# A linear-attention and MLP kernel: wider warm-up products, an earlier alpha load, 32-token denominator tiles, stores by tile and a new written-out order

## The chip, the cores and the metric

The kernel runs on one core of one Trainium2 chip. The metric is the device time of one execution in microseconds (us), lower is better. The kernel before takes 114.51 us, the median of three runs from 113.99 to 115.96 us.

## The reference

There are two stages. The first is attention without a softmax, for 4 batches, 4 heads, 1088 tokens and head size 32. Each query and key gets 64 features, the outer product of two projections to 8 numbers:

```python
a = np.einsum('rd,bhsd->bhsr', S1, x)
b = np.einsum('rd,bhsd->bhsr', S2, x)
phi = np.einsum('bhsi,bhsj->bhsij', a, b).reshape(*x.shape[:-1], r * r)
...
kv = np.einsum('bhsf,bhsd->bhfd', k_p, v)
z = np.sum(k_p, axis=2)
num = np.einsum('bhsf,bhfd->bhsd', q_p, kv)
den = np.einsum('bhsf,bhf->bhs', q_p, z)[..., None] + 1e-06
return (num / den).astype(np.float32)
```

The second takes the result as 4352 tokens of 128 numbers through an MLP of width 2048, whose activation is `max(h, 0) + alpha * min(h, 0)` with one alpha per hidden unit:

```python
h = x @ w_in
g = np.maximum(h, 0.0) + alpha * np.minimum(h, 0.0)
return (g @ w_out).astype(np.float32)
```

## The kernel before, in words

All work is cut into named operations, each with the engine it runs on. The string ORDER lists them in the order in which they are emitted, as `name:engine:buffers` (p is TensorE, a ScalarE, d VectorE, g GpSimd, s the SyncE queue of DMA issues). `arrange` walks this list, so each engine's instruction stream is the list read for that engine alone. An engine works strictly in its own order: an instruction that waits holds up everything behind it on that engine. This holds for SyncE too, which issues nearly all loads and all stores. At most eight DMAs are outstanding: a further one waits until the DMA that had its semaphore eight places earlier has landed. A number behind p (`zS0:p2`) asks for fill products: matmuls of constants into a scratch bank of PSUM, 128 columns each, four of them joined to one of 512.

The names that the prediction uses, for batch b:

- `ld_*` are the loads: k, q and v of each batch (k0 in two parts, q0 in two, each v in four pieces of 32 partitions), the rows of S1 and S2, alpha, two loads of w_in, four of w_out.
- `warm` is 104 small products of constants and some larger ones at the very start (line 276 on).
- Keys: `kbT` transposes k on VectorE, `kbf` projects it on TensorE (L484), `kbfT` transposes the projection (L489), `kbp0..` form the outer products (GpSimd or VectorE), `zsb` sums the features (L508), `kvb` contracts them with v (L519), and `kvc`, `fin`, `kvR` bring kv into the form that the queries need. For batch 0 `kw`, `kwT`, `kwc` do so by a short way.
- Queries of batch 0, first half, go by their own short way in two tiles i = 0, 1: `qaa`, `qab` (L576), `qac`, `qam`, then `den` (L585, L590), `rc` (reciprocal), `rT` (spreads it, L598), `rr`, `num` (L605) and `xA`, the first finished x. All other queries: `qbf`, `q1f` .. (L443), `..p0`, `..p1`, `..PT0`, `..PT1` (L544), `..n` (L551) and `..x0`, `..x1`.
- Since max(h,0) + alpha*min(h,0) = alpha*h + (1-alpha)*max(h,0), the MLP is x times W, with W = w_in times (alpha * w_out), plus ReLU(h) times w_a, with w_a = (1-alpha) * w_out. `alT` transposes alpha on TensorE (L335), `win` casts w_in to bf16, `w_a`, `w_b`, `w_hi`, `w_lo`, `winT`, `Wmm` make w_a and W. 
- The tokens go through the MLP in groups g = 0..9: `hg.c` is one 128-wide chunk of h for 512 tokens (L641; two chunks for 256 tokens), `rg.c` its ReLU into one of ten buffers, `og.c` the product with w_a into the group's PSUM bank (L664), `Wg` the product with W, `oTg` the transpose out of PSUM (L695) and `stg.i` the stores (L705). Group 9, the last 256 tokens, leaves the transpose out (L662, L677): `oT9.0` and `oT9.1` copy it from PSUM and one store (L723) writes it.

Of the kernel before, what the change touches and what calls it, by code (L numbers as in the profile page):

```python
# [11 lines left out]
F32 = mybir.dt.float32  # L12
# [10 lines left out]
wz:g ident:g eps:d pads9:g selP:g ld_rows_1:a M2:d zero:d M64:d M4:d M8b:d warm:p ld_k0.0:s ld_rows:a ld_k0.1:s M8i:d k0T0:d:0 MZ:g rowsT:p:0 pads:g  # L23
Wk:d S2m:p:1 table:a k0f0:p:2 Sab:a k0T1:d k0f1:p ld_qa:s S2q:d ld_k1:s qaT0:d qaa0:p:4 qab0:p Wf:a qaT1:d qaa1:p:0 qab1:p k0fT0:d:0 ld_v0_2:s
identb:g ld_alpha:a zs00:p:6 k0fT1:d qac0:a:0 k1T0:d:1 zs01:p z10:a:0 qam0:d k0p4:d:0 alT:p:2 oma:d ld_v0_3:s zS0:p2 alTc:d E8:g zA:d k0p1:g
k1f0:p1:3 k0p2:d ld_v0_1:s k0p0:g zfin:p:5 qac1:a:1 zc:d ld_v0:s kv00:p:2 k0p3:g kv01:p qam1:d k1fT0:d:1 kv02:p kv03:p kv04:p kw:a den0:p:5 kwT:p
kwc:a den1:p:0 rc0:d rT0:p ld_k2:s kvc0:a:0 fin0:p ld_w_in0:s k2T0:d:2 num0:p:1 k2f0:p:3 rc1:d rr0:a:0 win0:d rT1:p ld_qb:s xA0:d h0.0a:p:5 qbT:d
k1p1:g:1 win1:a kvR0:a rr1:a:1 num1:p:7 h0.2a:p:1 r0.0a:a:0 k2fT0:d:0 r0.2a:a:1 h0.4a:p:2 ld_w_in2:s r0.4a:a:2 C0:d h0.6a:p:0 xA1:d qbf:p:3 win3:d
win2:d zs10:p:7 r0.6a:a:3 h0.8a:p:1 h0.10a:p:2 k1p0:g h0.12a:p:0 qbfT:d:0 r0.10a:a:4 z11:a:1 h0.14a:p:3 h0.0b:p:4 qbt:d:0 qbrc:d:0 ld_w_out0:s
h0.2b:p:5 qbb:d w_b0:g qbp1:d:2 r0.0b:a:5 zs20:p:6 r0.12a:a:6 ld_w_out1:s z12:a:0 winT1:p:2 zS1:p ld_w_out3:s r0.8a:a:7 ld_w_out2:s h0.4b:p:4  # L30
r0.2b:d:8 C1:a qbp0:d w_a0:g w_a2:d zS2:p w_a1:g C2:d o0.0a:p:0 o0.2a:p h0.6b:p:1 w_a3:g r0.4b:a:9 r0.14a:a:0 h0.8b:p:7 h0.10b:p:5 o0.4a:p winT0:p:4
r0.8b:a:1 o0.6a:p r0.10b:a:2 winTc0:a h0.12b:p:3 r0.12b:a:3 h0.14b:p:7 o0.8a:p ld_q1:s o0.10a:p qbPT0:d:0 o0.12a:p w_b3:g w_b1:g ld_k3:s w_hi3:a
w_lo3:g qbPT1:d o0.14a:p o0.0b:p o0.2b:p r0.6b:d:7 qbn:p:3 winTc1:d o0.4b:p o0.6b:p o0.8b:p o0.10b:p o0.12b:p w_hi0:a w_lo0:g ld_v1_2:s qbx1:a qbx0:a
# [78 lines left out]
def kernel(  # L112
# [163 lines left out]
    def warm(e):  # L276
        for i in range(104):
            nc.tensor.matmul(PS[:32, 7, :16], ones(32), ones(16), start=True, stop=True, skip_group_check=True)  # L278
        dummy(16)
# [496 lines left out]
```

## Time and profile before

| | before |
|---|---|
| median of three runs | 114.51 us (113.99 to 115.96) |
| the profiled execution | 114.77 us |
| its span, first to last instruction | 112.3 us |
| TensorE busy / weight loads | 103.9 us / 60.9 us |
| VectorE, ScalarE, GpSimd busy | 82.7, 63.2, 43.0 us |
| DMA | 11.25 MB, mean 100 GB/s |
| chain that ended last | TensorE 87%, DMA 7% |

Between the span and the execution's own time lie 2.47 us. A busy TensorE is one that has a product in flight, not one at its peak, and the granted clock (PEclk) says at which speed it then works. The times in the timeline and in the chain of waits are us from the start of the span. Many matmuls in float32 stand in the trace as two records, so a count there can be twice the count in the program.

### The profile page before, as it was taken

Reading aid. Unit: us, or ns where it says so; the run is one execution under the profiler, and the core shown is the slowest. Engines: PE = TensorE matmul, PEld = TensorE weight load, DVE = VectorE, ACT = ScalarE, POOL = GpSimd, SP = SyncE. Lnnn points to the kernel's source line nnn. Section 1 sums busy time; section 2 is a strip of 40 time slices with the busy share of each in tenths; the row PEclk is TensorE's granted clock in tenths of the full one; section 3 lists DMA queues with packets and bytes.
Section 4 is the critical chain, followed back from the end, with each engine's and each line's share of the span. In section 5 each row is a group of like instructions: output and inputs, shape, how many; then the busy total and the mean of one; then the engine's idle time right before and its main releaser. Section 6 shows DMA issues by size and latency. Waiting matters only on the chain.

```text
span 112.3 us, 3587 instructions
## 1 busy us (share of the span) xinstructions
PE 103.9 (93%) x1520; PEld 60.9 (54%) x1520; DVE 82.7 (74%) x135; ACT 63.2 (56%) x128; POOL 43.0 (38%) x48
## 2 busy tenths in 40 slices
PE   7999499999999999999999999999999999999900
PEld 7444278636687567434444743444644446878700
DVE  4274584566999799789976985879999659678600
ACT  3112202417998777942966776499754957555400
POOL 4709109895305959997099500207000000000000
PEclk9999965559999999999999999999999999999996
DMA  3999999999950000030140100052006204312431
GB/s 95 252 269 230 355 346 325 329 243 266 286 121 3 6 3 6 0 67 3 22 71 0 29 0 6 0 101 39 6 0 105 41 0 83 57 17 49 71 64 42
DMA packets 23427, 11.25 MB, mean 100 GB/s; under 512 B 17636, under 2 KB 21876, under 8 KB 23412
## 3 DMA queue, kind: packets, MB, share of 16 engines
q1 hardware_dynamic: 23300, 11.01, 39.7%
q8 instruction: 12, 0.20, 0.7%
q10 hardware_dynamic: 112, 0.02, 0.1%
q14 instruction: 3, 0.02, 0.1%
HBM read 8.80 MB, written 2.23 MB: 98 GB/s over the span
## 4 chain that ended last, share of the span: by engine, by line
PE 87%; DMA 7%; DVE 1%; ACT 0%; issue 0%
PE ps L641 28%; PE ps L664 26%; DMA al<-in_moe_alpha_dram 7%; PE ps L551 5%; PE ps L519 5%; PE ps L278 3%; PE ps L443 2%; PE ps L484 2%; PE ps L274 2%; PE ps L598 2%; PE ps L590 2%; PE ps L385 2%; PE ps L662 2%; PE ps L605 1%; PE ps L403 1%; PE ps L375 1%
## 5 line engine op out<-in xcount | busy, mean ns | idle before, releaser
L641 PE MATMUL ps<-x,w_in_bf 128*128 128x512 bf16 (+1 forms) x176 | 40.1, 333 | 0.2
L641 PEld LDWEIGHTS <-w_in_bf 128*128 128x128 bf16 x176 | 16.5, 98 | 14.9 <-issue 3.6
L664 PEld LDWEIGHTS <-w_a_bf 128*128 128x128 bf16 x160 | 15.4, 98 | 10.7 <-issue 0.7
L186 POOL TENSOR_TENSOR P__72<-Fk__70 128x1024 f32<-128x1024 f32 (+1 forms) x4 | 8.6, 2166 | 6.4 <-DVE Fk__70 L489 6.4
L652 ACT ACTIVATE rh__86<-ps 128x512 bf16<-128x512 f32 x12 | 7.2, 600 | 5.0 <-PE ps L641 4.7
L652 ACT ACTIVATE rh__87<-ps 128x512 bf16<-128x512 f32 x12 | 7.2, 601 | 3.1 <-PE ps L641 3.0
L652 ACT ACTIVATE rh__83<-ps 128x512 bf16<-128x512 f32 x10 | 6.0, 600 | 3.0 <-issue 1.2
L186 POOL TENSOR_TENSOR w_hl<-w_in_f,w_hl 128x512 bf16<-128x512 f32 x4 | 4.6, 1158 | 7.3 <-ACT w_hl L179 6.0
L652 ACT ACTIVATE rh__82<-ps 128x512 bf16<-128x512 f32 x9 | 5.4, 600 | 1.6 <-PE ps L664 1.0
L652 ACT ACTIVATE rh__88<-ps 128x512 bf16<-128x512 f32 x10 | 6.0, 600 | 0.3 <-PE ps L664 0.3
L652 ACT ACTIVATE rh__89<-ps 128x512 bf16<-128x512 f32 x9 | 5.5, 607 | 1.1 <-PE ps L641 1.1
L652 ACT ACTIVATE rh__91<-ps 128x512 bf16<-128x512 f32 x9 | 5.5, 607 | 1.0 <-PE ps L641 1.0
L652 ACT ACTIVATE rh__85<-ps 128x512 bf16<-128x512 f32 x8 | 4.8, 601 | 1.9 <-PE ps L641 1.2
L652 ACT ACTIVATE rh__84<-ps 128x512 bf16<-128x512 f32 x9 | 5.5, 606 | 0.7 <-PE ps L641 0.4
L664 PE MATMUL ps<-rh__87,w_a_bf 128*128 128x512 bf16 (+1 forms) x18 | 5.3, 332 | 0.0
L664 PE MATMUL ps<-rh__85,w_a_bf 128*128 128x512 bf16 (+1 forms) x18 | 5.3, 332 | 0.0
L664 PE MATMUL ps<-rh__83,w_a_bf 128*128 128x256 bf16 (+1 forms) x19 | 5.3, 323 | 0.0
L664 PE MATMUL ps<-rh__88,w_a_bf 128*128 128x512 bf16 (+1 forms) x17 | 5.3, 342 | 0.0
L664 PE MATMUL ps<-rh__91,w_a_bf 128*128 128x512 bf16 (+1 forms) x16 | 5.0, 341 | 0.0
L664 PE MATMUL ps<-rh__89,w_a_bf 128*128 128x512 bf16 (+1 forms) x17 | 4.9, 329 | 0.0
L186 POOL TENSOR_TENSOR w_in_f<-w_out_f,alphaT 128x512 f32<-128x512 f32 x4 | 4.2, 1066 | 1.5 <-DVE w_in_bf L181 1.5
L179 ACT CAST x<-ps 128x576 bf16<-128x576 f32 (+1 forms) x5 | 2.7, 554 | 3.5 <-PE ps L551 3.3
(206 smaller groups left out, 231.1 us busy)
## 6 DMA issues: line engine op xcount, KB each, us to landing
v<-in_v_dram SPq DMA_DIRECT2D x12, 144.0 KB, 7.8
k<-in_k_dram SPq DMA_DIRECT2D x3, 544.0 KB, 7.9
q<-in_q_dram SPq DMA_DIRECT2D x3, 544.0 KB, 7.2
w_in_f<-in_moe_w_in_dram SPq DMA_DIRECT2D x2, 512.0 KB, 8.0
w_out_f<-in_moe_w_out_dram SPq DMA_DIRECT2D x4, 256.0 KB, 7.0
out_dram<-oT__92 SPq DMA_DIRECT2D x12, 64.0 KB, 1.9
out_dram<-oT__94 SPq DMA_DIRECT2D x8, 64.0 KB, 1.9
v<-in_v_dram SPq DMA_DIRECT2D x4, 112.0 KB, 7.8
```

The lines of the kernel that those rows point to most:

```text
L179: nc.scalar.copy(dst, src)
L186: (nc.vector if e == "dve" else nc.gpsimd).tensor_tensor(out=dst, in0=a, in1=b, op=what)
L274: nc.tensor.matmul(PS[:, 7, :m], ones(128), ones(m), start=True, stop=True, skip_group_check=True)
L278: nc.tensor.matmul(PS[:32, 7, :16], ones(32), ones(16), start=True, stop=True, skip_group_check=True)
L385: nc.tensor.matmul(ps(bw)[:, :DM], winT[:, c], w_hl[:, c, y], start=c == y == 0, stop=c == NC - 1 and y == 1)
L443: nc.tensor.matmul(ps(bf)[32 * g:32 * g + 32, h, :n], Wf[32 * h:32 * h + 32, b], src[1]()[32 * h:32 * h + 32, g * n:(g + 1) * n], start=Tr ...
L484: nc.tensor.matmul(ps(bf)[32 * g:32 * g + 32, u, :n], Wk[K].rearrange("p x f -> p (x f)"), src[1]()[K, g * n:g * n + n], start=True, stop= ...
L519: nc.tensor.matmul(ps(bk)[32 * h:32 * h + 32, :R], v_sb[b][:, h, j], bview(sb(P), [[1, R]], (4 * j + h) * R), start=j == 0, stop=j == JG - ...
L551: nc.tensor.matmul(ps(bn)[32 * h:32 * h + 32, g, :n], kvR[b][32 * g:32 * g + 32, y, 32 * h:32 * h + 32], bview(sb(Q)[32 * g:32 * g + 32], ...
L641: nc.tensor.matmul(ps(b)[:, n * i:n * i + n], w_in_bf[:, c], x(), start=True, stop=True, skip_group_check=len(cs) > 1)
L652: nc.scalar.activation(dst, src, ACTF.Relu)
L664: nc.tensor.matmul(ps(bo)[:, lo:lo + n], w, rhs, start=first and lo == 0, stop=end, skip_group_check=True)
```

## The change

- `warm`: the 104 small products have 32 columns instead of 16, and behind them come one product of 512 and three of 128 columns instead of four of 512.
- alpha is loaded on ScalarE's queue right behind the rows of S1 and S2, at the start, and `alT` stands ahead of the first `k0f`. Before, its load came after the copies `Sab` and `Wf`.
- v of batch 0 is issued ahead of all later loads, and k of batch 2 is now the second key batch to be worked on (k of batch 1 was). The new lists called `aft` only record which load comes behind which; nothing in the file reads them.
- `den`: the 128 tokens of a column block are cut in four tiles of 32 instead of two of 64.
- The group of the rest (the last two 32-token columns of every batch, 256 tokens) becomes group 6 and comes ahead of the first 512 tokens of the last batch, which become group 7.
- The stores of a group stand together, right behind its `oT`. The last store is cut in two halves of 64 partitions, one on SyncE and one on ScalarE.
- ORDER is new as a whole, with more fill products: 9 units ahead of `k0f0`, 7 ahead of `kv00` and 7 ahead of `k2f0`, 1 ahead of `alT`. Some costs written beside operations differ (they do no work).

```diff
-k1f0:p1:3 k0p2:d ld_v0_1:s k0p0:g zfin:p:5 qac1:a:1 zc:d ld_v0:s kv00:p:2 k0p3:g kv01:p qam1:d k1fT0:d:1 kv02:p kv03:p kv04:p kw:a den0:p:5 kwT:p
...
+ld_v3_3:s q1PT1:d:1 o0.14b:p W0:p r1.9:a:3 W1:p:1 oT0:d:0 st0.0:s st0.1:s st0.2:s st0.3:s ld_v1_1:s k1p0:g o1.0:p ld_v1_3:s o1.1:p kv10:p:2 ld_v3:s
...
-    oner = consts.tile([1, 64], F32, tag="oner", name="oner")
+    oner = consts.tile([1, 32], F32, tag="oner", name="oner")
...
     def warm(e):
         for i in range(104):
-            nc.tensor.matmul(PS[:32, 7, :16], ones(32), ones(16), start=True, stop=True, skip_group_check=True)
-        dummy(16)
-    op({"pe": 1760}, warm, name="warm")
+            nc.tensor.matmul(PS[:32, 7, :32], ones(32), ones(32), start=True, stop=True, skip_group_check=True)
+        dummy(7)
+    op({"pe": 1765}, warm, name="warm")
...
         def den(e, bd=bd, baq=baq):
-            for t in range(2):
-                nc.tensor.matmul(ps(bd)[64 * t:64 * t + 64, :8], oner, epsr, start=True, stop=False, skip_group_check=True)
+            for t in range(4):
+                nc.tensor.matmul(ps(bd)[32 * t:32 * t + 32, :8], oner, epsr, start=True, stop=False, skip_group_check=True)
             for c in range(2):
                 for u in range(2):
-                    for t in range(2):
-                        lo = 128 * c + 64 * t
-                        nc.tensor.matmul(ps(bd)[64 * t:64 * t + 64, 4 * c + 2 * u:4 * c + 2 * u + 2], sb(baq)[:, u, lo:lo + 64], zc[:, 2 * u:2 * u + 2],
+                    for t in range(4):
+                        lo = 128 * c + 32 * t
+                        nc.tensor.matmul(ps(bd)[32 * t:32 * t + 32, 4 * c + 2 * u:4 * c + 2 * u + 2], sb(baq)[:, u, lo:lo + 32], zc[:, 2 * u:2 * u + 2],
                                          start=False, stop=True, skip_group_check=True)
...
-            op({"sp": 600}, lambda e: nc.sync.dma_start(
-                bass.AP(tensor=out.tensor, offset=((B - 1) * S + lo // 32) * DM, ap=[[2 * DM, 4], [NJ * DM, 32], [1, 2 * DM]]),
-                t.rearrange("p j f -> p (j f)")), os, name=f"st{g}", nbytes=131072, rate=250.)
+            for j, en in enumerate(("sp", "act")):
+                op({en: 600}, lambda e, j=j: (nc.scalar if e == "act" else nc.sync).dma_start(
+                    bass.AP(tensor=out.tensor, offset=((B - 1) * S + lo // 32 + 4 * j) * DM, ap=[[2 * DM, 2], [NJ * DM, 32], [1, 2 * DM]]),
+                    t[64 * j:64 * j + 64].rearrange("p j f -> p (j f)")), os, name=f"st{g}.{j}", nbytes=65536, rate=250.)
...
-    for b in range(1, B):
+    for b in range(1, B - 1):
         mlp(g, [(512, cols(b, 0, 512), xs[b][:1])], store_main(b, 0, 512), True)
-        g += 1
-        if b < B - 1:
-            mlp(g, [(512, cols(b, 512, 512), xs[b])], store_main(b, 512, 512), True)
-            g += 1
+        mlp(g + 1, [(512, cols(b, 512, 512), xs[b])], store_main(b, 512, 512), True)
+        g += 2
     mlp(g, [(256, lambda: bview(x_sb, [[4 * JG * 32, B], [1, 64]], 1024), [o for b in range(B) for o in xs[b]])], store_rest, True)
+    g += 1
+    mlp(g, [(512, cols(B - 1, 0, 512), xs[B - 1][:1])], store_main(B - 1, 0, 512), True)
```

The new order, at three places. First SyncE's queue where the first store stands. Before, `v1_111` is v of batch 1, `v2_112` of batch 2, `v3_113` of batch 3, `oT0__92` the first group's output; one load is behind the first store, the last piece of v of batch 2:

```order
L192 DMA v1_111<-in_v_dram 32x4x288
L192 DMA v1_111<-in_v_dram 32x4x224
L192 DMA v1_111<-in_v_dram 32x4x288 x2
L192 DMA v2_112<-in_v_dram 32x4x288
L192 DMA v3_113<-in_v_dram 32x4x288
L192 DMA q2_116<-in_q_dram 128x1088
```

```order
L192 DMA v2_112<-in_v_dram 32x4x288
L192 DMA v3_113<-in_v_dram 32x4x224
L705 DMA out_0_dram<-oT0__92 32x16x32
L192 DMA v2_112<-in_v_dram 32x4x224
L705 DMA out_0_dram<-oT1__93 32x16x32
L705 DMA out_0_dram<-oT0__92 32x16x32 x3
```

The same place of the queue in the changed kernel:

```order
L193 DMA q2_116<-in_q_dram 128x1088
L193 DMA v1_111<-in_v_dram 32x4x288 x2
L193 DMA v3_113<-in_v_dram 32x4x224
L710 DMA out_0_dram<-oT0__92 32x16x32 x4
L193 DMA v1_111<-in_v_dram 32x4x288
L193 DMA v1_111<-in_v_dram 32x4x224
L193 DMA v3_113<-in_v_dram 32x4x288
L193 DMA k0_107<-in_k_dram 128x1088
L193 DMA v3_113<-in_v_dram 32x4x288
L193 DMA q0_114<-in_q_dram 128x1088
L710 DMA out_0_dram<-oT1__93 32x16x32 x4
```

Two of the four pieces of v of batch 1 have moved behind the four stores of group 0, with two of v and the k and q of batch 3 (`k0_107` and `q0_114` are reused for it).

On TensorE, `kv10`, which reads all four pieces of v of batch 1, stands in the changed kernel three products behind `W0`, the product that completes group 0 (two rows of 256 columns):

```order
L669 MATMUL ps_63<-x_150,W_bf_139 128x256
L669 LDWEIGHTS W_bf_139
L669 MATMUL ps_63<-x_150,W_bf_139 128x256
L669 LDWEIGHTS W_bf_139
L669 MATMUL ps_63<-x_150,W_bf_139 128x512
L669 LDWEIGHTS w_a_bf_137
L669 MATMUL ps_63<-rh5__87,w_a_bf_137 128x512
L669 LDWEIGHTS w_a_bf_137
L669 MATMUL ps_63<-rh7__89,w_a_bf_137 128x512
L524 MATMUL ps_63<-P0__71,v1_111 32x64 x36
```

Before, it stood among the first chunks of group 1, ahead of `Wmm` and of `W0`:

```order
L641 LDWEIGHTS w_in_bf_136
L641 MATMUL ps_63<-x_150,w_in_bf_136 128x512
L641 LDWEIGHTS w_in_bf_136
L641 MATMUL ps_63<-x_150,w_in_bf_136 128x512
L519 MATMUL ps_63<-P1__72,v1_111 32x64 x36
L385 LDWEIGHTS winT_140
L385 MATMUL ps_63<-w_hl_138,winT_140 128x128
```

So `kv10` has moved behind the first group's last product. At the start of TensorE's work the first product of the MLP came behind these rows before (`al_103` is alpha, `T1__65` and `T2__66` the transposed keys of batches 1 and 2, `rd8_152` the reciprocals):

```order
L335 MATMUL ps_63<-ident_119,al_103 128x16
...
L484 MATMUL ps_63<-T1__65,Wk_129 32x288 x8
L426 MATMUL ps_63<-zA_147,E8_124 128x32
L519 MATMUL ps_63<-P0__71,v0_110 32x64 x36
```

```order
L598 MATMUL ps_63<-ident_119,rd8_152 32x128 x8
L403 MATMUL ps_63<-ident_119,kvs0__80 128x128 x2
L605 MATMUL ps_63<-aq0__98,kv0W_146 32x256 x4
L484 MATMUL ps_63<-T2__66,Wk_129 32x288 x8
L598 MATMUL ps_63<-ident_119,rd8_152 32x128 x8
```

In the changed kernel, where `T1__65` holds the keys of batch 2:

```order
L524 MATMUL ps_63<-P0__71,v0_110 32x64 x28
...
L489 MATMUL ps_63<-T1__65,Wk_129 32x288 x8
L414 MATMUL ps_63<-ident_119,kv0c_145 128x128
L603 MATMUL ps_63<-ident_119,rd8_152 32x128 x8
L610 MATMUL ps_63<-aq0__98,kv0W_146 32x256 x4
L590 MATMUL ps_63<-epsr_134,oner_135 32x8 x4
L595 MATMUL ps_63<-zc_149,aq1__99 32x2 x16
L423 MATMUL ps_63<-z10__96,S2q_104 32x8 x4
```

One projection of keys (batch 1), one `rT`, `fin0` and `num1` have moved behind the first product of the MLP, and the projection of batch 2 now stands between `kv0` and the short way to the first x.

More of the change, by code (lines that the diff above doesn't have):

```diff
@@ L27 @@
[L27 to L30, printed above, removed]
@@ L85, in __init__ @@
         self.deps = [d for d in deps if d is not None]
+        self.aft = []
         self.on, self.fill = None, 0
@@ L234 @@
     load_v(0)
+    early = got("k0.0") + got("k0.1") + got("qa") + got("v0")
+    for x, y in zip(early, early[1:]):
+        y.aft = [x]
     load_rows("qb", q_sb[0][:, 16:], q, 0, 16, NJ - 16)
```

94 lines of the change are left out of this document (51 added, 43 removed).

## The prediction

> **What bounds the kernel now.** The page comes first: who is busy, and when.
>
> ```profile
> span 112.3 us, 3587 instructions
> PE 103.9 (93%) x1520; PEld 60.9 (54%) x1520; DVE 82.7 (74%) x135; ACT 63.2 (56%) x128; POOL 43.0 (38%) x48
> ```
>
> ```profile
> PEclk9999965559999999999999999999999999999996
> ```
>
> TensorE is busy 93% of the span, so it sets the time. The last row has the span in 40 slices of 2.81 us; the clock that TensorE is granted is low from slice 6 to 9, about 14 to 25 us. The clock changes in the trace at three points (11.48 up, 14.90 down, 25.14 up), so I asked the view of stretches for pieces of 3.41 us around these, and for two long ones. Its columns are the busy time and count of PE, weight loads, DVE, ACT and POOL, then clock, DMA share and GB/s.
>
> ```profile
> 8.07:11.48 3.41, 3.41 (x40) 1.58 (x36) 1.95 (x4) 0.58 (x1) 3.05 (x3) 1.00 1.08 234
> 11.48:14.90 3.42, 1.85 (x48) 1.05 (x48) 1.97 (x7) 0.67 (x2) 0.05 (x1) 1.00 1.01 373
> 14.90:18.31 3.41, 3.41 (x92) 3.15 (x94) 1.68 (x5) 0.27 (x1) 1.27 (x1) 0.50 1.17 317
> 21.72:25.14 3.42, 3.42 (x43) 1.36 (x42) 1.86 (x4) 0.98 (x3) 3.42 (x4) 0.50 1.09 241
> 25.14:28.55 3.41, 3.37 (x75) 1.98 (x74) 2.21 (x5) 2.84 (x7) 2.26 (x3) 1.00 1.02 284
> 23.00:47.30 24.30, 24.13 (x445) 15.21 (x433) 21.14 (x32) 19.06 (x41) 15.73 (x13) 0.96 0.41 102
> 45.00:106.50 61.50, 61.45 (x751) 33.12 (x748) 50.71 (x74) 40.93 (x79) 17.47 (x10) 1.00 0.20 35
> ```
>
> ```profile
> 3.64 1.89 PE L274 MATMUL ps<-const-bfloat16-1.0 128*128 128x512 bf16 x4
> ```
>
> ```profile
> 57.65 0.86 PE ps L641 x4
> ```
>
> Before 11.48 the trace has no record of the clock, and the views then print 1.00; the products tell otherwise: four warm-up ones of 512 columns took 1.89 us (0.47 each), four of 512 in the MLP later 0.86. So the start runs at half the clock too. After 11.48 it reads so: one stretch in which TensorE was busy for 1.85 of 3.42 us is followed by half the clock, and only a stretch full of wide products (21.72 on) brings it back. From 45.0 to 106.5 PE is busy 61.45 of 61.50 us at full clock: nothing there can be gained by an order, only by less work. The gains lie ahead of 45 us. The hole in the second stretch is in the chain of waits and in the timeline:
>
> ```profile
> 6.01 7.30 DMA al<-in_moe_alpha_dram
> ```
>
> ```profile
> 13.36 0.23 PE L335 MATMUL ps<-ident,al 16*128 16x16 f32 x1 [1.57 <-DMA al<-in_moe_alpha_dram]
> ```
>
> TensorE stood 1.57 us for alpha, whose transfer took 7.30 us behind the big loads.
>
> **The change, part by part: the start.** In the timeline of the queues and of VectorE:
>
> ```profile
> 0.75 0.92 ACTq L192 DMA_DIRECT2D rows<-in_S_dram  x2
> ```
>
> ```profile
> 2.15 0.43 SPq L192 DMA_DIRECT2D k<-in_k_dram  x1
> 2.63 1.91 SPq L192 DMA_DIRECT2D v<-in_v_dram  x4
> ```
>
> ```profile
> 10.20 1.31 DVE L453 STREAM_TRANSPOSE T__65<-k 128x1088 f32<-128x1088 f32 x1 [1.46 <-DMA k<-in_k_dram]
> 16.19 0.77 DVE L489 STREAM_TRANSPOSE Fk__70<-ps 128x576 f32<-128x576 f32 x1
> 18.62 0.21 DVE L593 RECIPROCAL rd<-ps 128x8 f32<-128x8 f32 x1 [1.65 <-PE ps L590]
> 23.02 0.43 DVE L607 TENSOR_TENSOR x<-ps,rr__100 128x256 bf16<-128x256 f32 x1 [1.41 <-PE ps L605]
> 26.38 0.75 DVE L181 CAST w_in_bf<-w_in_f 128x512 bf16<-128x512 f32 x2
> ```
>
> ```profile
> k<-in_k_dram SPq DMA_DIRECT2D x3, 544.0 KB, 7.9
> ```
>
> ```profile
> DMA to landing us min/median/max: 6.4/8.0/9.5
> ```
>
> The first of these two is k's, the second that of w_in.
>
> alpha now follows the two rows, at about 0.75 + 0.92 = 1.67 us. With the 3 to 4 us that I give it (its 7.30 is from a queue already loaded) it is there by 6, beside k0, and the 1.57 us go. What is late next is the second key batch: it now stands behind the four pieces of v, so it is issued at 2.15 + 1.91 + 0.43, about 4.6, and lands 7.9 later, at 12.5. Then VectorE does strictly in turn its transpose (1.31, to 13.8), `rc0` (0.21, to 14.0), `win0`, `Wf`, `S2q`, `k2fT0` and `xA0`. w_in is issued at 5.1 and lands 8.0 later, at 13.1; the cast is half of 0.75 for one of two, 0.4, and I end it between 14.4 and 15.0, the latter where the load takes a us longer. With 0.2 each for `Wf` and `S2q` (as `rc0`) and 0.77 for the transpose, `xA0` begins at **16.2** (15.6 to 17.5, the late end at half clock) and not at 23.02: some 6.8 us earlier.
>
> The four-tile `den` has 40 records for 20. Its price is open: the old ones are these in the chain, at half clock.
>
> ```profile
> 17.30 0.32 PE ps L585 x4
> 17.62 0.95 PE ps L590 x16
> ```
>
> Doubled, 1.3 us each; below, nothing, since small products on different rows may overlap (the sum of features takes 0.31 for 18 at full clock). Neither end counts in the sum: `den0` runs while VectorE waits for k2, `den1` beside VectorE's work after `xA0`. The 23 fill products stand in waits too. If that cover is gone, 1.3 us is the cost. Warm-up of 32 columns touches only the clock (first rival).
>
> **From the first x to the first group's end.** Two engines can set this. TensorE: it had its first h products at 24.85 and had finished group 0's products and `o1.0` at 45.0, so 20.15 us of work; the new order leaves one `rT` (1.0 at half clock, so 0.5), one `fin0` (0.2) and one key projection (0.7) for after that point, 1.4 us, while `kv10` for `kv20` and the later chunks change places. From 16.7 this gives 16.7 + 20.15 + 1.4 = 38.3.
>
> ```profile
> 24.85 0.48 PE ps L641 x2
> ```
>
> ```profile
> 44.38 2.16 PE ps L664 x11
> ```
>
> VectorE: before 23.02 to 47.32, of which 21.14 us busy. Out of the stretch go three ReLUs, the two casts of w_in (0.75), one key transpose, one product of features and q1's second transpose:
>
> ```profile
> 31.03 0.68 DVE L654 TENSOR_SCALAR rh__90<-ps 128x512 bf16<-128x512 f32 x1
> 43.99 1.38 DVE L544 STREAM_TRANSPOSE Q__75<-P__71 128x1152 f32<-128x1152 f32 x1
> 47.32 0.67 DVE L695 STREAM_TRANSPOSE oT__92<-ps 128x512 f32<-128x512 f32 x1
> ```
>
> 3 x 0.68 + 0.75 + 1.31 (as above) + 0.68 (the product, as wide as a ReLU) + 1.38 = 6.16. In come a key transpose (1.31), `rc1` (0.21) and `rr1`, `qbx0`, `q1b` (0.4 each, as the 256-wide x), three casts `w_hi` (0.4 each, as those of w_in), two `w_lo` and a ReLU (512 wide, 0.68 each): 5.96. So the busy time stays at 20.9, and the idle 3.16 us may stay or shrink to nothing: from 16.2, 37.1 to 40.3. I take **38.2** for `oT0`, where both agree.
>
> **The stores and `kv10`.** This is the part that speaks against the change.
>
> ```profile
> 48.02 0.33 SPq L705 DMA_DIRECT2D out_dram<-oT__92  x1
> ...
> 55.25 1.59 SPq L705 DMA_DIRECT2D out_dram<-oT__92  x3
> ```
>
> ```profile
> k<-in_k_dram SPq DMA_DIRECT2D x1, 288.0 KB, 3.0
> ```
>
> ```profile
> out_dram<-oT__92 SPq DMA_DIRECT2D x12, 64.0 KB, 1.9
> ```
>
> Two pieces of v of batch 1 now wait on SyncE behind the four stores, which wait for `oT0`. The second piece's issue begins at 38.2 + 0.67 + 0.33 + 1.59 + 0.43 (a load's issue, as k's above) = 41.2. A piece of 144 KB lands between the 1.9 of a small store and the 3.0 of 288 KB on a free queue; 2.5 gives 43.7, with the gaps between issues **43.8**. TensorE has three products after `W0` (0.22 each, some 0.65 us), so it is ready for `kv10` at 38.2 + 0.65, and stands still for **5 us** (4.3 to 6). Queued behind it on TensorE is everything. ScalarE and VectorE run out soon after.
>
> Before, the point of equal work left lay at 45.0; now it lies at 43.8. So of 6 us won ahead of it **1.2** is left. But a hole of 5 us is three times the one of 1.57 that cost the clock. At half clock for one or two stretches of 3.41 us TensorE does 1.7 or 3.4 us less work; I take **2.6**, bounds 0 (the stretches fall well, and the fall is not taken) and 4.4.
>
> **The other stores and the end.** Elsewhere the loads behind a group's stores are wanted 10 us or more later, so 0. Groups 6 and 7 changing places costs the same products: 0. At the end:
>
> ```profile
> 106.49 0.27 ACT L179 COPY of<-ps 128x128 f32<-128x128 f32 x1 [1.20 <-PE ps L662]
> 107.81 0.69 SPq L723 DMA_DIRECT2D out_dram<-of  x1
> ```
>
> ```profile
> SPq L771 <- DMA out_dram<-of: 2.7, 1, 2.7
> ```
>
> The last copy ended at 106.76, and the store was issued only 1.05 later, since SyncE was still at other stores; the new order has them out of the way: -1.05. The halves may each take as long, half as long or, if each half finds fewer DMA engines, twice as long: of the 2.7 us of waiting all but the issue's 0.69 is transfer, 2.0, so -1.0, 0 or +2.0. While it ran, the DMA share was low:
>
> ```profile
> 109.00:110.00 1.00, 0.00 (x0) 0.00 (x0) 0.00 (x0) 0.00 (x0) 0.00 (x0) 1.00 0.23 55
> ```
>
> 0.23 of 16 engines is 3.7, as many as the pattern's first dimension, 4; that of a half is 2, so I lean upwards, to +0.7: in all **-0.35**. [...]
>
> **Sum**, against the profiled execution: 114.77 - 1.2 + 2.6 - 0.35 = 115.8. That execution is 0.26 above the median of 114.51, so **115.5**.
>
> **The rivals.** *The clock does not hold at the start (slower).* With 16 columns the clock rose only after the stretch from 8.07. If 32 columns don't change this, or the wait for k2 between small products (until 12.5) costs it as alpha's wait did, `xA0` moves to 17.5 (+1.3), and the work after it is at half clock for 3.4 to 6.8 us, 1.7 to 3.4 lost; VectorE hides the smaller part: 115.5 + 1.3 + 1.7, to 119.9, say **118.5**. It decides as soon as a 3.41 us stretch between 8 and 25 us shows half clock. For it: the stretch from 14.90, busy all through with small products, didn't raise the clock. Against: the new warm-up products are twice as wide. 0.25. [...]
>
> *alpha comes late all the same (slower).* If its 7.30 us don't shrink, it lands at 9.0, and `alT` stands ahead of `k0f0` in TensorE's order, so all of the keys' chain shifts by some 3 us, of which the wait for k2 hides a part: + 2.5, **118**. 0.08.
>
> *The stall is shorter (faster).* If w_in and k2 land after 6.4 as the quickest load of its size does, `xA0` begins near 14.6, `oT0` at 36.6, and with 1.9 to land `kv10` starts at 41.6: 3.4 us ahead of before, less 1.7 for the clock, less 2.05 at the end (halves at half the time): 114.77 - 3.4 + 1.7 - 2.05 = 111.0, **110.8** on the median's scale. With no stall at all it would be 114.8 - 6.1 - 0.35, near 108. For it: less DMA traffic is ahead of w_in than before. Against: DMA share is 1.0 until 28 us. 0.20.
>
> **How the numbers follow.** Forecast 0.47, clock 0.25, alpha 0.08, short stall 0.20. The forecast's own range is 113.2 (clock lost once, halves no slower) to 116.8. What a measurement can tell is about 2%, 112.2 and 116.8: faster takes the short stall, 0.20; slower the two others, 0.33; the rest 0.47. The range reaches into both sides until one in ten is left on each: 111.0 to 119.3.
>
> **What would show it.** Right: `alT` without a wait; full clock from about 11 us on; `xA0` near 16; `oT0` near 38; on TensorE one idle time of about 5 us before `kv10`, released by a v load of SyncE's queue, with a digit 5 of the clock after it. Wrong: no idle time there (then near 108), or a low clock between 8 and 25 us as before (then near 118.5); or a last wait on the store over 4 us.

## The result, and the profile after

The changed kernel takes 125.95 us (median of 4 runs, 123.29 to 127.04), the kernel before beside it 114.25 us: a ratio of 1.09, 95% interval 1.0667 to 1.1133. It is slower by 9%, where the prediction had 115.5 and a range up to 119.3. The ratios in this text leave disturbed executions out and the medians don't, so the two need not divide exactly; where a kernel has no interval, too few executions were undisturbed.

The page of the changed kernel, profiled at 127.04 us, answers to the first rows of the prediction:

```profile
span 124.6 us, 3677 instructions
...
PE 102.2 (82%) x1555; PEld 61.0 (49%) x1569; DVE 83.7 (67%) x137; ACT 64.6 (52%) x131; POOL 43.7 (35%) x46
...
PE   7899775599999382068999999999999999999900
...
PEclk9999999657999959555899999999999999999995
```

TensorE is no longer busy all through: it is at 5 tenths near 20 us, and at 3, 8, 2 and 0 between 40 and 53 us (a slice is 3.1 us). The clock is up earlier than before, but it falls three times. Four points divide the span: the first x, the first group's transpose `oT0`, the start of `kv10`, after which both kernels have the same work left on TensorE (before: the point at 45.0), and TensorE's end.

| stretch | before, us | changed, us | difference | predicted |
|---|---|---|---|---|
| to the first x | 23.02 | 14.76 | -8.3 | -6.8 |
| first x to `oT0` | 24.30 | 33.26 | +9.0 | -2.3 |
| `oT0` to the point of equal work | -2.32 | 6.06 | +8.4 | +7.9 |
| from there to TensorE's end | 61.45 | 64.10 | +2.7 | +2.6 |
| TensorE's end to the end of the span | 5.82 | 6.46 | +0.6 | -0.35 |
| sum | 112.3 | 124.6 | +12.3 | +1.0 |

(Stretches of before and after, from the two timelines; the predicted differences from the points that the prediction names.) One row is wrong by 11 us, the others by 1.5 or less each.

**The start** went better than forecast. In TensorE's and VectorE's timelines, whose rows begin with the start and the duration and end with the idle time before them and what ended it:

```profile
4.94 0.28 PE L340 MATMUL ps<-ident,al 16*128 16x16 f32 x1
14.76 0.42 DVE L612 TENSOR_TENSOR x<-ps,rr__100 128x256 bf16<-128x256 f32 x1 [0.64 <-PE ps L610]
```

**From there to `oT0`** VectorE was idle for 8.9 us of 33.3, and busy for longer (the columns of the view of stretches are those of the prediction):

```profile
14.76:48.02 33.26, 25.81 (x470) 17.51 (x470) 24.40 (x34) 19.30 (x44) 21.54 (x14) 0.85 0.36 90
```

TensorE has two holes there for which the profile shows no cause; "issue" as a releaser means that it waited for nothing that the profile shows:

```profile
16.28 0.23 PE L590 MATMUL ps<-epsr,oner 1*32 1x8 f32 x5 [1.51 <-issue]
23.30 0.48 PE L513 MATMUL ps<-Fk__70 128*32 128x32 f32 x17 [2.75 <-issue]
```

Both cut a row of like products in two: three of eight records of `den1` run, then nothing for 1.51 us, then the other five. And two of VectorE's products are longer than their like: `w_lo3` takes 2.86 us where `w_lo1` took 0.69, and q1's second product 3.32 where the kernel before had 1.36. VectorE first, then GpSimd at that time, then TensorE, which waits for `w_lo3`:

```profile
34.67 0.69 DVE L187 TENSOR_TENSOR w_hl<-w_in_f,w_hl 128x512 bf16<-128x512 f32 x1
...
40.10 2.86 DVE L187 TENSOR_TENSOR w_hl<-w_in_f,w_hl 128x512 bf16<-128x512 f32 x1
42.88 3.32 DVE L187 TENSOR_TENSOR P__73<-F__68 128x1152 f32<-128x1152 f32 x1
```

```profile
39.82 2.59 POOL L187 TENSOR_TENSOR P__71<-Fk__69 128x1280 f32<-128x1280 f32 x1
42.38 2.61 POOL L187 TENSOR_TENSOR P__73<-F__68 128x1152 f32<-128x1152 f32 x1
```

```profile
43.01 0.85 PE L390 MATMUL ps<-w_hl,winT 128*128 128x128 bf16 x7 [2.00 <-DVE w_hl L187]
```

The first of the two long ones (`w_lo3`) begins after GpSimd's product and ends 0.55 us after GpSimd's has ended (42.41); the second begins after GpSimd's second and ends 1.21 after that one's end (44.99). So I read it that 0.55 and 1.2 is what they take, and that the rest is waiting; e2_port, below, tests this.

**The wait before `kv10`** is there as forecast. TensorE, SyncE's queue, and the chain of waits:

```profile
54.08 2.15 PE L524 MATMUL ps<-P__71,v 128*32 128x64 f32 x72 [6.41 <-DMA v<-in_v_dram]
```

```profile
48.72 1.96 SPq L710 DMA_DIRECT2D out_dram<-oT__92  x4
50.71 1.45 SPq L193 DMA_DIRECT2D v<-in_v_dram  x3
```

```profile
51.73 2.36 DMA v<-in_v_dram
```

`oT0`, four stores, then the loads, and 6.41 us without a product. Behind it the clock is at half from 49.94 to 60.18, and full from there:

```profile
50.00:60.20 10.20, 5.79 (x112) 3.56 (x113) 1.47 (x2) 1.94 (x4) 0.00 (x0) 0.50 0.65 185
60.20:117.50 57.30, 56.56 (x637) 30.43 (x629) 45.04 (x68) 38.53 (x72) 14.26 (x8) 1.00 0.18 32
```

**The end**: the store is issued 0.07 us after the copy, but waited for longer than before (4.1 us in two waits, the longest 3.1, for 2.7 in one). While the two halves were on their way the DMA share was 0.13 of 16 engines, which is 2; the whole store had 0.23, which is 3.7.

```profile
118.59 0.68 SPq L729 DMA_DIRECT2D out_dram<-of  x1
```

```profile
SPq L780 <- DMA out_dram<-of: 4.1, 2, 3.1
```

```profile
120.00:121.00 1.00, 0.00 (x0) 0.00 (x0) 0.00 (x0) 0.00 (x0) 0.00 (x0) 1.00 0.13 30
```

### The profile page after: what moved, and what is told of

Same layout as the page of the kernel before. It is cut to its first block, busy times and chain, and to the rows that moved or that the text cites. A ratio compares the mean times of both kernels' runs of the same rounds, so it can differ in the third digit from the quotient of the medians.

```text
span 124.6 us, 3677 instructions
## 1 busy us (share of the span) xinstructions
PE 102.2 (82%) x1555; PEld 61.0 (49%) x1569; DVE 83.7 (67%) x137; ACT 64.6 (52%) x131; POOL 43.7 (35%) x46
## 3 DMA queue, kind: packets, MB, share of 16 engines
HBM read 8.80 MB, written 2.23 MB: 88 GB/s over the span
## 4 chain that ended last, share of the span: by engine, by line
PE 69%; DVE 12%; issue 6%; DMA 5%; SPq 3%
PE ps L646 24%; PE ps L669 24%; PE ps L556 5%; PE ps L524 4%; DMA q<-in_q_dram 3%; DVE P__73 L187 3%; PE ps L448 2%; DVE w_hl L187 2%; DMA v<-in_v_dram 2%; PE ps L489 2%; SPq L710 1%; PE ps L667 1%; SPq L193 1%; DVE F__68 L451 1%; PE ps L513 1%
## 5 line engine op out<-in xcount | busy, mean ns | idle before, releaser
L646 PE MATMUL ps<-x,w_in_bf 128*128 128x512 bf16 (+1 forms) x171 | 41.3, 352 | 0.4 <-DVE F__68 L451 0.2
L182 DVE CAST x<-ps 128x576 bf16<-128x576 f32 (+1 forms) x4 | 2.8, 691 | 15.4 <-PE ps L556 15.4
L524 PE MATMUL ps<-P__71,v 128*32 128x64 f32 x216 | 4.8, 251 | 6.4 <-DMA v<-in_v_dram 6.4
L187 POOL TENSOR_TENSOR P__71<-Fk__69 128x512 f32<-128x512 f32 (+3 forms) x6 | 8.7, 1464 | 3.3 <-DVE Fk__69 L494 3.3
L657 ACT ACTIVATE rh__82<-ps 128x512 bf16<-128x512 f32 x10 | 6.0, 598 | 4.5 <-PE ps L646 4.0
L657 ACT ACTIVATE rh__86<-ps 128x512 bf16<-128x512 f32 x12 | 7.3, 606 | 1.8 <-PE ps L646 1.8
L524 PEld LDWEIGHTS ps<-P__71,v 128*32 128x32 f32 x216 | 4.1, 130 | 7.5 <-issue 6.9
L657 ACT ACTIVATE rh__87<-ps 128x512 bf16<-128x512 f32 x11 | 6.5, 595 | 2.1 <-PE ps L669 1.7
L657 ACT ACTIVATE rh__89<-ps 128x512 bf16<-128x512 f32 x11 | 6.7, 605 | 1.3 <-PE ps L646 1.0
L657 ACT ACTIVATE rh__83<-ps 128x512 bf16<-128x512 f32 x11 | 6.6, 598 | 1.2 <-PE ps L646 1.0
L187 POOL TENSOR_TENSOR P__73<-F__68 128x1152 f32<-128x1152 f32 x3 | 6.9, 2313 | 0.1
L657 ACT ACTIVATE rh__91<-ps 128x512 bf16<-128x512 f32 x10 | 6.0, 604 | 1.4 <-PE ps L669 0.7
L657 ACT ACTIVATE rh__90<-ps 128x512 bf16<-128x512 f32 x9 | 5.4, 602 | 2.1 <-PE ps L646 2.0
L657 ACT ACTIVATE rh__84<-ps 128x512 bf16<-128x512 f32 x9 | 5.4, 600 | 1.8 <-PE ps L646 1.8
L549 DVE STREAM_TRANSPOSE Q__75<-P__73 128x1152 f32<-128x1152 f32 x4 | 5.4, 1354 | 0.0
L669 PE MATMUL ps<-rh__82,w_a_bf 128*128 128x512 bf16 (+1 forms) x17 | 5.2, 347 | 0.0
L187 POOL TENSOR_TENSOR P__72<-Fk__70 128x1024 f32<-128x1024 f32 (+1 forms) x2 | 4.3, 2156 | 2.8 <-DVE Fk__70 L494 2.8
```

Source lines behind the costliest of these rows:

```text
L182: nc.vector.tensor_copy(dst, src)
L187: (nc.vector if e == "dve" else nc.gpsimd).tensor_tensor(out=dst, in0=a, in1=b, op=what)
L524: nc.tensor.matmul(ps(bk)[32 * h:32 * h + 32, :R], v_sb[b][:, h, j], bview(sb(P), [[1, R]], (4 * j + h) * R), start=j == 0, stop=j == JG - ...
L549: ts.append(op({"dve": V(R * half) + 20}, lambda e, x=x: nc.vector.transpose(bview(sb(Q), [[1, R * half]], x * R * half), bview(sb(P), [[1 ...
L646: nc.tensor.matmul(ps(b)[:, n * i:n * i + n], w_in_bf[:, c], x(), start=True, stop=True, skip_group_check=len(cs) > 1)
L657: nc.scalar.activation(dst, src, ACTF.Relu)
```

## The experiments

Three costs stand against the change: the stores ahead of loads (S), products on VectorE and GpSimd that seem to exclude each other (P; 2.86 us for `w_lo3` beside GpSimd's product, 0.69 for `w_lo1`), and holes in TensorE's stream, for which I took the arrival of its own instructions as the cause (H). The trace of the changed kernel has 12 transfers of instructions, 16384 bytes each, on a queue of their own (packets, MB, share of 16 engines):

```profile
q8 instruction: 12, 0.20, 0.7%
```

The runs were taken in rounds, each with the kernel before beside it (median 113.5 us for e1 to e4, 114.55 for e5 to e8, 114.04 for e9 to e11); a ratio is to the kernel before of the same round.

**The loads ahead of the stores (e1_loads).**

```diff
-... oT0:d:0 st0.0:s st0.1:s st0.2:s st0.3:s ld_v1_1:s k1p0:g o1.0:p ld_v1_3:s o1.1:p ...
+... oT0:d:0 ld_v1_1:s ld_v1_3:s st0.0:s st0.1:s st0.2:s st0.3:s k1p0:g o1.0:p o1.1:p ...
```

> The changed kernel, with the two pieces of v of batch 1 issued ahead of the four stores of group 0 and not behind them; nothing else is touched. Theory S (stores ahead of loads): the wait of 6.4 us before kv10 goes, and with it the half clock after it (about 2.6 us), so 7 to 9 us are won and the median falls from about 125 to 116-118. Rival (the time went before kv10, in the instruction-fetch holes and in VectorE's long products; without the loads TensorE would wait there for something else): the idle time gets another releaser and less than 2 us are won.

Measured: 116.55 us (113.35 to 116.89) beside 113.5 for the kernel before. In TensorE's timeline `kv10` follows at once:

```profile
45.00 0.63 PE L669 MATMUL ps<-rh__89,w_a_bf 128*128 128x512 bf16 x1
45.56 2.15 PE L524 MATMUL ps<-P__71,v 128*32 128x64 f32 x72
```

9.4 us by the medians for two words of the order (9.9 between the shortest executions): S holds, at a little more than the 7 to 9 us that I gave. The clock is now full from 47.78 on and not from 60.18. `oT0` still begins only at 45.36, 30.0 us behind the first x.

**One product moved to GpSimd (e2_port).**

```diff
-... w_lo0:g q1rc:d:1 q1b:d w_lo3:d w_lo2:g ...
+... w_lo0:g q1rc:d:1 q1b:d w_lo2:g w_lo3:g ...
```

> The changed kernel, with one product (w_lo3) moved from VectorE to GpSimd, behind w_lo2. Theory P (VectorE's and GpSimd's products of two SBUF operands exclude each other): w_lo3 took 2.86 us on VectorE beside GpSimd's 128x1280 product where w_lo1 took 0.69 alone; gone from VectorE, q1's second product of 128x1152 begins 2.8 us earlier and then takes about 1.2 instead of 3.3 if it meets GpSimd's w_lo3 alone; oT0 comes 3 to 5 us earlier, and as kv10 hangs on oT0 the median falls by 3 to 5, to 120-122. Rival (VectorE was slowed by something else, for example DMA or its own operands): the second product still takes 3.3 and less than 2.5 us are won.

Measured: 119.61 us, ratio 1.0551 (1.0439 to 1.0663). The ratio was 1.09 for the changed kernel, so about 4 us are won, as forecast (3 to 5); the medians, 6.3 us apart, make more of it. `oT0` begins at 43.88 instead of 48.02. VectorE and GpSimd:

```profile
39.87 2.20 DVE L187 TENSOR_TENSOR P__73<-F__68 128x1152 f32<-128x1152 f32 x1
```

```profile
38.24 2.61 POOL L187 TENSOR_TENSOR w_hl<-w_in_f,w_hl 128x512 bf16<-128x512 f32 x2 [1.56 <-DVE w_hl L182]
40.81 3.49 POOL L187 TENSOR_TENSOR P__71<-Fk__69 128x1280 f32<-128x1280 f32 x1
```

GpSimd's pair, `w_lo3` second, ends at 40.85; VectorE's product ends 1.22 later, at 42.07; GpSimd's next, begun at 40.81, ends 2.23 after that (44.30) and took 3.49 for the 2.59 of the other trace. (That 2.59 has a wait in it too: it ends 2.23 after VectorE's product that began at 39.69 and took 0.49.) In both traces it looks as if one of the two is served whole while the other waits: VectorE's products ended 0.55, 1.21 and 1.22 us after GpSimd's, GpSimd's 2.23 us after VectorE's, twice. So P holds, in both directions; what makes the two exclude each other, no run shows. The stall before `kv10` is the same here (6.79 us), as it should be.

**Fewer warm-up instructions (e3_warm52).**

```diff
-        for i in range(104):
-            nc.tensor.matmul(PS[:32, 7, :32], ones(32), ones(32), ...
+        for i in range(52):
+            nc.tensor.matmul(PS[:32, 7, :64], ones(32), ones(64), ...
```

> The changed kernel, with the 104 warm-up products of 32 columns made 52 of 64 columns: some 104 instructions fewer ahead of everything else on TensorE, about the same work. Theory H (the holes of 1.5 us at 14.8 and 2.75 us at 20.6, which have no releaser, are waits for TensorE's own instructions, which come in blocks of 16 KB): the holes move to places about 100 records later in the program or go, and the transfers of instructions move with them; time by that between -4 and +2. Rival (the holes belong to these products, the ones of den1 and zs20, or to the data traffic at that time): they stay at the same lines with the same length, and the time stays within 1 us.

Measured: 125.31 us, ratio 1.0966 (1.0833 to 1.1099), no change in time. But the holes have moved:

```profile
12.34 0.64 PE L524 MATMUL ps<-P__71,v 128*32 128x64 f32 x27 [1.01 <-issue]
19.01 0.27 PE L408 MATMUL ps<-ident,kvs__80 128*128 128x128 f32 x1 [1.96 <-issue]
```

They are in `kv0` and in `fin0` now, and none is left in `den1` or `zs20`. The transfers of instructions stand beside them each time (us from the span's start; the last column counts TensorE's products that began before the hole):

```
kernel          transfer of instructions   hole on TensorE          products before
changed         13.6 to 14.8               14.78 to 16.28, den1     345
changed         20.6 to 21.8               20.55 to 23.30, zs20     473
e3_warm52       10.0 to 11.1               11.33 to 12.34, kv0      221
e3_warm52       16.4 to 17.6               17.05 to 19.01, fin0     348
e11_warm26      13.6 to 14.8               13.81 to 16.16, kv0      221
e9_den64        21.6 to 22.9               21.97 to 24.35, zs10     476
```

Each hole of the table begins around a transfer and ends 1.3 to 1.5 us after it. The last column is the strongest sign: whatever stands there, a hole comes after 221, 348 or 476 products (the changed kernel's own trace, with 345 and 473, lacks a few records: 1555 products in all, for 1569 in e7_unsplit), and in e1, e2 and e4 to e8 the holes of over 1 us come after 348 or 476 as well. That is a step of 127 or 128 products with as many weight loads, some 256 records, and a program with fewer records ahead has another operation at that place. So H holds, as a reading: TensorE runs out of instructions. The views themselves name no releaser for these holes. The hole of `den1` has moved to `fin0`, about as far behind as warm-up products are gone (52), as forecast; the one in `kv0` is at a place that the changed kernel passes without a hole, and the third transfer (20.6 to 21.7) leaves none of over 0.3 us here. So not every transfer leaves a hole. Those from 25.4 on in the changed kernel leave none of over 0.2 us; the products there are wider and take longer each, which would fit, but no run tests it.

**The warm-up of before (e4_warm16).**

```diff
-            nc.tensor.matmul(PS[:32, 7, :32], ones(32), ones(32), ...
-        dummy(7)
+            nc.tensor.matmul(PS[:32, 7, :16], ones(32), ones(16), ...
+        dummy(16)
```

> The changed kernel, with the warm-up as it was before: 104 products of 16 columns and four of 512. Theory W (the wider warm-up products raised the clock at 5.6 us): the clock rises one or two windows of 3.41 us later, at 9 or 12.4, the first x comes 1 to 3 us later, the time is up to 3 us longer. Rival (what kept the clock low in the kernel before was the wait for alpha alone): the clock rises at about the same time, and the time stays within 1 us.

Measured: 125.07 us (two executions), ratio 1.1061 (1.0948 to 1.1175). The clock rose at 7.14 instead of 5.57, the first x came at 16.00 instead of 14.76, and the time stayed. The us at the first x need not be the clock's: four products of 512 columns took 1.89 us here, so TensorE came to the transpose of `rows` at 5.45 instead of 4.51. Nor is the clock's own part clear, for with the products of 32 columns it rose anywhere from 3.41 (e1_loads) to 6.22 (e9_den64). `oT0` is even earlier, 46.18 for 48.02: the second hole, 1.66 us long, was not followed by half the clock here, which stayed full until 41.28. That the clock holds at the start without the wide products speaks for alpha; e8_before_alpha tests that by itself.

**Both edits (e5_both).** The first two diffs together.

> The changed kernel with both edits: the two pieces of v of batch 1 ahead of the first stores, and w_lo3 on GpSimd. Theory (stall and port exclusion are two costs, one behind the other): the gains add, 8 to 9 from the loads and 4 to 5 from the product: about 110-113, at or under the kernel before. Rival (they lie beside each other, so the one hides the other): 115-116, as with the loads alone.

Measured: 113.24 us, ratio 0.9829 (0.9741 to 0.9916), just outside the forecast. The gains add for the most part: 12.7 us by the medians, about 12 by the ratios, for the 9.4 and the 4 of the two alone.

**The last store in quarters (e6_quarters), and whole (e7_unsplit).** On top of both edits:

```diff
-            for j, en in enumerate(("sp", "act")):
+            for j, en in enumerate(("sp", "act", "sp", "act")):
...
-                    bass.AP(tensor=out.tensor, offset=((B - 1) * S + lo // 32 + 4 * j) * DM, ap=[[2 * DM, 2], [NJ * DM, 32], [1, 2 * DM]]),
-                    t[64 * j:64 * j + 64].rearrange("p j f -> p (j f)")), os, name=f"st{g}.{j}", nbytes=65536, rate=250.)
+                    bass.AP(tensor=out.tensor, offset=((B - 1) * S + lo // 32 + 2 * j) * DM, ap=[[NJ * DM, 32], [1, 2 * DM]]),
+                    t[32 * j:32 * j + 32].rearrange("p j f -> p (j f)")), os, name=f"st{g}.{j}", nbytes=32768, rate=250.)
```

> As the kernel with both edits, and the last store cut in four quarters of 32 partitions, two on SyncE and two on ScalarE, instead of two halves of 64. From the issue of the last store to the end of the span it was 4.5 us before (one store) and 6.0 in the changed kernel (two halves). [...] Rival (the end is a fixed latency of each DMA, and every further one adds to it): 6 us or more, no gain.

and, whole, as before the change:

```diff
-            for j, en in enumerate(("sp", "act")):
...
+            op({"sp": 600}, lambda e: nc.sync.dma_start(
+                bass.AP(tensor=out.tensor, offset=((B - 1) * S + lo // 32) * DM, ap=[[2 * DM, 4], [NJ * DM, 32], [1, 2 * DM]]),
+                t.rearrange("p j f -> p (j f)")), os, name=f"st{g}", nbytes=131072, rate=250.)
```

> As the kernel with both edits, and the last store whole, on SyncE, as it was before the change. Theory (halves go out at half the rate): issue to end is 4.5 us as before, 1.5 less than with the halves, and the time falls by 1 to 1.5. Rival (the halves cost nothing and the longer end is chance): same within 0.5.

Measured: quarters 110.08 us, ratio 0.9579 (0.951 to 0.9647); whole 111.57 us, ratio 0.964 (0.9541 to 0.9739). SyncE's issue and last wait, first of the quarters, then of the whole store:

```profile
104.67 0.80 SPq L729 DMA_DIRECT2D out_dram<-of  x2
```

```profile
SPq L780 <- DMA out_dram<-of: 1.3, 1, 1.3
```

```profile
104.72 0.69 SPq L728 DMA_DIRECT2D out_dram<-of  x1
```

```profile
SPq L779 <- DMA out_dram<-of: 2.7, 1, 2.7
```

From the first issue to the end of the span: halves 6.0 us (e5_both, from 104.87 to 110.9), whole 4.5, quarters 3.2. The forecasts were 3 to 4 for the quarters and 4.5 for the whole. The three times don't follow the bytes in a piece (64, 128 and 32 KB), but they fall as the first dimension of the pattern grows: 2, 4, 32. The DMA share goes with this for two of them, 0.13 for the halves (2 engines for both together) and 0.23 for the whole store of the kernel before (3.7); how many engines carried the quarters, no run shows. e6_quarters has the lowest ratio of this study: without S and P, and with the store in quarters, the new order is 4% faster than the kernel before.

**The kernel before, with alpha early (e8_before_alpha).**

```diff
-... ld_rows:a ld_k0.1:s ... identb:g ld_alpha:a zs00:p:6 ...
+... ld_rows:a ld_alpha:a ld_k0.1:s ... identb:g zs00:p:6 ...
```

> The kernel before, with one word of its order moved: the load of alpha is issued right behind the second of the rows of S1 and S2. Theory (alpha's wait of 1.57 us cost the clock from 14.9 to 25.1 as well): the idle time goes, the clock stays up once it has risen, and the first x comes 2 to 4 us earlier than 23.0; 2 to 5 us less in all. Rival (the clock rises late anyway because the early products are small, or the second key batch comes no earlier): under 1.5 us.

Measured: 112.65 us, ratio 0.9792 (0.972 to 0.9864), a gain of 1.9 us by the medians and 2.4 by the ratio, at the low end of the forecast. The wait has gone, the clock stays full from 9.17 on, and the first x is 4.9 us earlier:

```profile
10.62 0.23 PE L335 MATMUL ps<-ident,al 16*128 16x16 f32 x1
```

```profile
18.08 0.42 DVE L607 TENSOR_TENSOR x<-ps,rr__100 128x256 bf16<-128x256 f32 x1 [0.84 <-PE ps L605]
```

At `oT0` only 2.1 of the 4.9 are left (45.18 for 47.32). At full clock the kernel before now has holes of its own, of which it had none:

```profile
19.78 0.71 PE L484 MATMUL ps<-T__66,Wk 64*32 64x288 f32 x14 [1.37 <-issue]
...
27.62 0.49 PE L375 MATMUL ps<-identb,w_in_bf 128*128 128x128 bf16 x6 [1.38 <-issue]
```

**den in two tiles (e9_den64).** On top of e6_quarters:

```diff
-            for t in range(4):
-                nc.tensor.matmul(ps(bd)[32 * t:32 * t + 32, :8], oner, epsr, start=True, stop=False, skip_group_check=True)
+            for t in range(2):
+                nc.tensor.matmul(ps(bd)[64 * t:64 * t + 64, :8], oner, epsr, start=True, stop=False, skip_group_check=True)
```

and the loop over the products likewise; `oner` is 64 wide again.

> As the kernel with the loads ahead, w_lo3 on GpSimd and the last store in quarters (110.08 us), and den in two tiles of 64 tokens again, as before the change: 40 fewer records on TensorE over den0 and den1. The prediction put this edit at 0. If it is 0: within 0.7 us. If the small products lie on the path (rival): 0.5 to 1.3 less per den. With fewer records the hole at den1 (1.6 us) should move by some 20 to 40 records behind it, if it is a wait for instructions.

Measured: 109.97 us (107.83 to 110.45) for 110.08 (109.5 to 112.56): no cost seen, as the prediction had it, though the executions lie too far apart to rule out a price under a us. The trace settles the price that the prediction left open: at full clock `den0` in two tiles took 0.85 us (20 records), in four tiles 0.61 (40 records, e6_quarters), so the four tiles are cheaper and not twice as dear. Of the 1.61 us that e6_quarters lost in `den1`, 0.49 are left, at 16.96 in the products behind `den1` (L423): 20 products or 40 records further on, as forecast, and again after 348 products. The long hole is now at the next place, after 476 products, where e6_quarters had 0.56:

```profile
24.35 0.23 PE L513 MATMUL ps<-Fk__69 128*32 128x32 f32 x3 [2.38 <-issue]
```

**Two ideas of the change in the old order (e10_before_plus).** The edit of e8_before_alpha, and the quarters, in the kernel before.

> The kernel before with two of the change's ideas alone: alpha loaded early (112.65 us by itself) and the last store cut, but in four quarters on two queues; its old order otherwise. Theory (these are small, separate gains that need no new order): the end shrinks by 1.4 as from whole to quarters, perhaps 0.5 more since ScalarE's half is not behind SyncE's other stores: 110.5 to 111.3. Rival (the quarters wait behind the stores that SyncE still has to issue, which the new order cleared): 112 to 112.6, no gain.

Measured: 110.68 us, inside the forecast, but the kernel before was 0.5 us faster in this round, and the ratio, 0.9781 (0.9663 to 0.9898), is that of e8_before_alpha alone (0.9792). So the times don't show that the quarters gained anything here. SyncE's two quarters were issued at 106.47, 2.1 us after the copies had ended (104.38), behind other stores, as the rival has it; in the trace some 0.6 us of the quarters' gain are left (copy's end to the span's end 4.9 for 5.5).

**Fewer instructions still (e11_warm26).** On top of e6_quarters, 26 warm-up products of 128 columns:

```diff
-        for i in range(104):
-            nc.tensor.matmul(PS[:32, 7, :32], ones(32), ones(32), ...
+        for i in range(26):
+            nc.tensor.matmul(PS[:32, 7, :128], ones(32), ones(128), ...
```

> As the kernel with the loads ahead, w_lo3 on GpSimd and the last store in quarters, and the warm-up of 26 products of 128 columns instead of 104 of 32: some 156 records fewer, the same time of work. Theory H (holes come from blocks of instructions): the transfers of instructions come later and the hole moves from den1 (15.2 us) to a place 100 to 200 records behind; what it costs depends on what waits there: -1.6 to +1. Rival (the hole belongs to den1): it stays at den1 with 1.4 to 1.9 us.

Measured: 112.54 us, ratio 0.989 (0.9724 to 1.0055), 2.5 us worse than e6_quarters and outside what I gave. `den1` has no hole any more, but the hole did not go to a place behind it, as I expected: it is in `kv0`, ahead of it, after 221 products, as in e3_warm52. The transfer beside it is the first of this kernel; in e6_quarters the first one came at 5.0 to 5.9 and left no hole. The hole in e11_warm26, and its first x:

```profile
16.16 0.22 PE L524 MATMUL ps<-P__71,v 128*32 128x64 f32 x1 [2.34 <-issue]
```

```profile
20.55 0.42 DVE L612 TENSOR_TENSOR x<-ps,rr__100 128x256 bf16<-128x256 f32 x1 [1.65 <-PE ps L610]
```

`kv0` is on the path to the first x, which came at 20.55 for 15.21. Not all of these 5.3 us are the hole's: the clock rose only at 10.00 (4.99 in e6_quarters), and TensorE was 1.3 us behind when `kv0` began (11.62 for 10.33). The hole itself is 2.3, and the rest, 1.7, goes with the half clock from 16.83 to 20.24 behind it.

## Why the prediction was wrong

**The start: right, a size off.** alpha came without a wait, and the clock rose at 5.57 and held until 22.63. k2 was there when VectorE was free for it, at 10.49; the 7.9 us to landing that I took from the median row were under 6.3. So -8.3 for -6.8.

**First x to the first group's end: the step that failed.** I wrote: "So the busy time stays at 20.9, and the idle 3.16 us may stay or shrink to nothing". VectorE's busy time was 24.40, and its idle time 8.9. For the busy time I took durations of before as if an operation had one duration; but two that I counted (`w_lo`, 0.68) or left as they were (q1's second product) now met GpSimd's products, and 4.1 us of waiting came in (2.86 - 0.69 and 3.32 - 1.36). e2_port shows it: with `w_lo3` away VectorE's busy time in the stretch is 20.9. The trace of before had it in view, VectorE first, then GpSimd:

```profile
42.60 1.36 DVE L186 TENSOR_TENSOR P__71<-F__68 128x1152 f32<-128x1152 f32 x1
```

```profile
42.64 3.34 POOL L186 TENSOR_TENSOR P__71<-F__68 128x1152 f32<-128x1152 f32 x1
```

GpSimd's 128x1152 product took 3.34 us there beside VectorE's of 1.36, and 2.61 in the changed kernel.

For the idle time I let it stay at 3.16 or shrink, and for TensorE I counted 20.15 + 1.4 us of work and no time in which it stands still. It stood still for 4.3 us in the two holes and for 2.00 behind the late `w_lo3`, and after the second hole the clock was at half from 22.63 to 29.46, up to 3.4 us of work; VectorE waited behind that. That the holes come from the arrival of instructions is read from the places at which they come: after 221, 348 or 476 products, whatever stands there (e3, e9, e11). Two traces with almost the same holes tell what each cost. The same stretch in e4_warm16, with `w_lo3` still on VectorE, holes of 2.10 and 1.66 us and full clock until 41.28, and in e7_unsplit, with `w_lo3` away, holes of 1.41 and 2.48 us and full clock all through:

```profile
16.00:46.18 30.18, 23.35 (x472) 15.96 (x470) 25.09 (x34) 18.98 (x44) 21.75 (x14) 0.94 0.36 90
```

```profile
15.21:41.72 26.51, 21.77 (x472) 15.34 (x470) 21.25 (x33) 18.88 (x44) 20.98 (x14) 1.00 0.48 119
```

So of the 33.3 us some 3.1 go with the clock lost behind the second hole (33.3 to 30.2), 3.7 with the products that exclude each other and what hangs on them (30.2 to 26.5; e1_loads and e5_both, 30.0 and 26.6, give 3.4), and 4.5 are left against the 22.0 that I forecast. I put these down to the holes and the waits behind them, but only by difference: e11_warm26, whose hole lies ahead of its first x, took 23.6 for the stretch, yet it starts it 5.3 us later, with more done.

**The stores and `kv10`: right.** Four stores took 1.96 (1.92 forecast), the second load landed 2.8 us after its issue began (2.5), the hole was 6.4 us (4.3 to 6), the loss to the clock 2.7 (2.6). The clock was at half for three stretches and not one or two, but 4.1 us of these lay in the wait itself. e1_loads took the wait and the half clock behind it away. I had set this cost against 6 us won ahead of it; of the 8.3 us won by the first x nothing was left at `oT0`.

**The end: one half right.** Clearing SyncE's queue gave 0.98 (1.05 forecast). The halves cost 1.6, where I took 0.7 from between -1.0 and +2.0, although the row that I quoted (3.7 engines busy for a first dimension of 4) said already which bound was the likely one: both halves together had 2 engines (a DMA share of 0.13).

**The rivals.** The clock that doesn't hold at the start did not come, nor did the late alpha. (Half the clock from 22.63 on touches the sign that I gave for the first of them, 8 to 25 us, but it follows a hole that I had not forecast; and by its own terms that rival's upper end is 115.5 + 1.3 + 3.4, 120.2 and not 119.9.) The short stall's premise, loads that land sooner, did come, and the first x with it; its end did not, since it shared the failed step. None of the rivals was a wait inside the first group's stretch, and the range, made from the rivals, ended 4 us below the fastest run.

## What to carry to other kernels

When an order is written anew, a duration read from the old trace may hold only beside the same neighbours (a product of 128x512 took 0.69 and 2.86 us here): look for the rows where the same operation took two different times, and ask which other engine was busy then. A load that must land soon doesn't belong behind stores that wait for a result, on the same queue; two words of the order were worth 9 us here. And before cutting a last store in pieces, look at which dimension comes first in its pattern: here halves with 2 in front were slower than the whole with 4 (6.0 us for 4.5), and quarters with 32 in front took more than a quarter off its end (3.2).

## What the runs showed of the hardware that I had not expected

TensorE seems to run out of instructions. In stretches of small products at full clock, holes of 1.01 (e3_warm52) to 2.75 us (the changed kernel) opened in the middle of rows of like products, beside transfers of instructions and always after 221, 348 or 476 products, 127 or 128 apart. At half clock, in the kernel before, there was none: from 14.90 to 25.14 TensorE was busy all through (10.24 of 10.24 us), with one of the transfers at 18.1 to 19.2. Warm-up products count among these records, so changing them moves the holes: with 52 fewer, the one in `den1` came in `fin0` (e3_warm52).

A short idle time was followed by half the clock in some of these traces and not in others. The clock changes in them on a grid of 3.41 us (half from 18.64 to 22.06 in e6_quarters, and for two such pieces, 22.63 to 29.46, in the changed kernel). A hole of 1.61 us that lay in one piece of the grid was followed by half clock in e6_quarters (15.23 to 16.84, clock down at 18.64), and one of 2.48 us in e7_unsplit, which the grid cuts in two pieces of under 1.3 us, was not (20.90 to 23.38, cut at 22.16). But where a hole falls on the grid does not settle it alone: in e4_warm16 one of 1.66 us lay in one piece (22.38 to 24.04; the piece is 20.79 to 24.21) and was not followed by half clock, though TensorE was busy for only 1.76 us of that piece, against 1.80 in the piece of e6_quarters.
